# A linear-attention and mixture kernel: u spread by a bf16 product, no dummy products, another division of small work, and all orders anew

## The chip, the core and the metric

The kernel runs on one core of a Trainium2 chip. A core has five engines, each with an instruction queue of its own that it works through strictly in order: TensorE (PE, matrix products and transposes), VectorE (DVE), ScalarE (ACT), GpSimd (POOL) and SyncE (SP, which here only issues transfers). Transfers between the chip's main memory and the core's buffers, and transposes by transfer, run on 16 DMA engines that all queues share. The metric is the device time of one execution in microseconds (us).

## What is computed

Two stages follow each other. The first is a linear recurrence over 768 positions for 4 batches of 8 heads with 48 channels; the second is a feed-forward stage over the 3072 resulting rows of 384 numbers, with 1024 hidden columns.

```python
# first stage: r, k, v, w are [4, 8, 768, 48], u is [8, 48]; the state is [48, 48] per batch and head
for t in range(768):
    cur   = outer(u * k[t], v[t])
    y[t]  = r[t] @ (state + cur)
    state = w[t][:, None] * state + outer(k[t], v[t])
# second stage: x is y as [3072, 384]
h    = x @ w_in                                   # 1024 columns
solu = h * softmax(h)
ln   = (solu - mean(solu)) / sqrt(var(solu) + 1e-6) * g_ln
out  = ln @ w_out
```

The term with `u` is a bonus of each position for itself: the sum over the 48 channels of r·k·u, a single number per position and head, times the row v.

## The kernel before, in words

The positions are cut into 6 chunks of 128. A chunk of one batch is a **unit**; unit `i` is chunk `i // 4` of batch `i % 4`, so there are 24 units, and units 0 to 3 have no state behind them. For each unit the program does the following, and each step is one **word** in an order written out by hand:

- `LW`, `LK`, `LR`, `LV` load w, k, r and v of the unit (192 KB each). The ending of the word names the queue that issues the transfer: none is SP, `.a` is ACT, `.g` is POOL. `LI` and `LO` load the weights, `LU` and `LG` load u and the gain.
- `lw` (ACT) takes the logarithm of w, `cum` (PE, two products of 384 columns) sums it along the chunk, `ex` (ACT) takes exponentials, `kp` (DVE) multiplies them into k and r.
- The scaled k and r are turned, either by PE (`krk` and `krr`, eight transposes of 128 columns in all, copied out by `kr.a` on ACT or `kr.d` on DVE) or by a transfer (`kt`, issued by SP).
- `M` (PE) makes the scores, `m` masks them (DVE; `m.a` with `sel` in two units is ACT and POOL).
- `p` and `q` (POOL) make r·k and r·k·u; `dg` (DVE) sums q per head; `vb` casts v to bf16 on ACT or POOL; `dv` (POOL) multiplies the bonus by v.
- `Y` (PE) makes the attention output. With `.i` and a bank number, PE also adds `dv` by a product with the identity, and ACT copies the result out (`y.a`); with `.n`, DVE adds `dv` while it copies out (`y.d`).
- `S` (PE), `et` (ACT) and `st` (DVE) make the new state.
- y is turned, by PE (`X`, copied out by `xT.a` or `xT.d`) or by a transfer (`xt`, issued by SP).
- `H` (PE, 24 products of 128 columns) makes the hidden rows, `e` (ACT) exponentials, `he` (DVE) h·e, `hq` (ACT) its square. `Oa` and `Ob` (PE, four blocks each) multiply by w_out, and beside it sum the exponentials and the squares with products of two columns and one column. For units with `ea`, POOL first adds the two halves of the exponentials, which halves the number of those products. In units with `ht`, H is made by rows (six products of 512 columns), the two sums come from ACT's accumulators, and a transfer turns the result.
- `qm`, `lv`, `rs`, `o`, `out` normalise the rows and store them.

Before the first `H`, w_in must be cast to bf16 (`wi0` to `wi2`), and w_out must be scaled by the gain (`gw`) and centred (`mn`, `mc`, `ce`). `ih` and `ik` build constants. `hot` is a series of products whose result nobody reads.

What sets the order of the work is the string `ORDER` alone: it is walked word by word, and each engine gets its instructions in that order (class `InOrder`, lines 70 to 97; lines 680 to 683). An instruction that must wait therefore holds up everything behind it on its engine. A digit at the end of a PE word is the PSUM bank. Rings of buffers limit how far an engine can run ahead: seven loaded units, four to ten of the others (line 67). The trace has one line, 86, for nearly all instructions, because `InOrder.call` issues them; groups are told apart by the tiles that they write and read.

u is spread over all 128 rows by one product with a row of ones, in f32, before `q` can use it:

```python
u_row = consts.tile([1, DM], F32)                                                          # line 167
pe.matmul(ps["u"], lhsT=ones_row, rhs=u_row, start=True, stop=True)                        # us, line 279
act.copy(out=u_bc.rearrange("t h d -> t (h d)"), in_=ps["u"])                              # uc
```

Of the kernel before, what the change touches and what calls it, by code (L numbers as in the profile page):

```python
# [8 lines left out]
F32 = mybir.dt.float32  # L9
BF16 = mybir.dt.bfloat16  # L10
# [11 lines left out]
LU0 LR3.g LW3.a LW1.a LW2.g lw3 LR0.a cum3.0 LG0 ih0 ex3 LW0 gs0.7 LK3 LR2.g hot1.2 LV0.g ik0 LK0 lw1 lw0 LV3.g  # L22
gc0 cum0.4 LK2.a us0.6 p0 lw2 LW5.g ex0 kp3 LR1 kp0 cum1.0 cum2.2 krk3.7 krr3 uc0 ex2 q0 ex1 kp2 LK1 LR6.g kp1
krk0.6 LW4 krr0 krk2.5 krr2 kr0.a lw4 LR4.g vb0.a kr2.d vb3.a p1 M0.3 p3 LO0 LW6 dg0 M2.5 kr3.a LK4 m0.d lw5
hot10.1 LV1 LR5 LK6.a dv0 LK5.g m2.d LV2.a LO1 M3.0 S0.7 q3 gw2.a gw3.a hot1.4 LI1 q1 lw6 krk1.6 cum4.2 et0 LV4
m3.d p2 st0 cum6.0 dg3 gw0.a cum5.4 ex4 S3.7 gw1.a p4 kp4 q2 dv3 krr1 ex6 dg1 LV5.g krk4.3 krr4 ex5 vb1.a Y0.i2
kp6 kr4.d y0.a LI2 et3 X0.2 krk6.3 st3 p6 kr1.a vb2.a LW8 xT0.a kp5 krr6 LI0.a dg2 M1.0 krk5.7 krr5 kr6.a m1.d
S1.2 dv1 M4.4 dv2 Y3.i3 S2.6 gw4.a LK7 gw7.a et2 kr5.d LW7.g et1 m4.d hot1.7 y3.a gw5.a gw6.a p5 LR7.g M6.0
vb5.p Y2.i7 Y1.n3 vb4.a mn0.4 wi1.a y2.a st1 LW11.a wi0.p mc0 m6.d st2 S4.5 X3.2 LW10 y1.d et4 wi2.p ce0.d xT3.a
S5.0 ce5.p X1.7 LW9.a LV7.g et5 X2.6 M5.2 lw7 st5 st4 cum7.0 xT2.a H0.5 xT1.a LR10 lw8 ex7 m5.d ce1.d e0 H1.2  # L30
LR8 kp7 q5 he0 H3.0 q4 LV8.a ce3.p lw10 dg5 ce7.p ce6.p krk7.5 dg4 LK10 H2.6 LK8.a LV11 ce2.p krr7 LV6 e1 Y4.n4
he1 hq0.a LW13.a e3 e2 ce4.p dv4 he3 Oa0.3 cum10.1 he2 kr7.d y4.d Ob0 p7 cum8.6 qm0 lw11 hq1.a dv5 Oa1.0 ex10
Y5.n5 kp10 LR11 y5.d p8 LK11.a LK13 LW15 Ob1 X4.5 ex8 M7.1 lv0 krk10.4 rs0 kp8 q6 o0.a LK9.a vb6.p LW12 LR9 qm1
# [18 lines left out]
o11.a Oa10.5 kp20 e13 dv16 M17.0 out11 ea13.p he13 dg19 cum22.2 e15 p20 ex22 dv17 Y16.i4 he15 Ob10 kp22 y16.a
H14.6 hq13.a e14 qm10 LW23.g q20 p22 M18.3 dv18 q22 ea15.p S18.2 LV20 lv10 kt19 m17.d Y17.n1 m18.d hq15.a Oa13.0
y17.d et18 dg20 st18 Ob13 rs10 he14 M19.3 ea14.p o10.a xt16 vb20.p qm13 H16.1 e16 kt22 dv20 Y18.n6 X17.5 m19.d
lv13 kt20 y18.d out10 xT17.a q21 rs13 Oa15.7 LV22.g Ob15 he16 M20.4 qm15 hq14.a S17.3 lv15 m20.d H17.1 dg21 et17
st17 kt21 M21.5 dv19 rs15 LR23 o15.a e17 m21.d Oa14.4 Ob14 he17 lw23 o13.a qm14 cum23.5 Y19.n3 xt18 Y20.n7 ex23
y19.d lv14 out15 y20.d ht16 LV23 ea17.p vb22.p rs14 vb21.a o14.a H18.0 p23 e18 X20.2 dg22 M22.3 S19.7 hq17.a
kp23 xT20.d m22.d Oa16.6 sv16 dv21 Y21.n5 hq16.a sv18 vb23.a Ob16 sq16 et19 H20.2 out13 he18 q23 y21.d dg23 dv22
e20 st19 xt19 he20 H19.0 Y22.n5 Oa17.7 kt23 e19 dv23 qm16 Ob17 y22.d ht18 M23.4 xt21 he19 lv16 rs16 o16.d Oa18.3
Ob18 hq20.a H21.0 hq18.a hq19.a m23.d ht20 xt22 out14 sq18 sv20 qm18 e21 lv18 ea19.p Y23.n2 rs18 Oa19.6 qm17  # L60
ea21.p lv17 rs17 y23.d Ob19 he21 Oa20.5 hq21.a qm19 out16 H22.0 o17.d xt23 lv19 o18.d rs19 Oa21.2 HA23.3 Ob21
# [39 lines left out]
def kernel(  # L101
# [14 lines left out]
    C = 128  # L116
# [50 lines left out]
    u_row = consts.tile([1, DM], F32)  # L167
# [29 lines left out]
    ones_row = consts.tile([1, C], F32)  # L197
    dve.memset(ones_row, 1.0)
# [37 lines left out]
    u_bc = consts.tile([C, H, D], BF16)  # L236
    gr = consts.tile([128, KF], F32)
# [38 lines left out]
    def load_u(i, x):  # L276
        queue[x].dma_start(out=u_row, in_=u.rearrange("(o h) d -> o (h d)", o=1))
# [11 lines left out]

    def spread_u(i, x):  # L290
        ps["u"] = bank([C, DM], F32, x, "u_ps")
        pe.matmul(ps["u"], lhsT=ones_row, rhs=u_row, start=True, stop=True)
# [421 lines left out]
```

## Time and profile before

| | |
|---|---|
| median of three runs | 143.97 us (143.61 to 146.4) |
| the profiled execution | 142.83 us, of which the span of the trace is 141.0 us |
| PE busy | 125.5 us, 89% |
| DVE busy | 122.3 us, 87% |
| ACT busy | 118.9 us, 84% |
| POOL busy | 118.3 us, 84% |
| moved by DMA | 31.98 MB, 227 GB/s in the mean |

A group row of the trace reads: line, engine, operation, tiles out<-in, shapes, count | busy us, mean ns of one | idle time of the engine just ahead of them and what ended it. A row of the timeline reads: start, duration, engine, line, operation, tiles, count and, in brackets, the engine's wait ahead of it. Products are pipelined: the duration of one runs until its result has landed, so what a product costs a busy PE is read from start to start. All four engines are busy in more than eight tenths of the span, so a row's share says little; what matters is which of them the others wait for in a stretch.

### The profile page before, as it was taken

The page shows a single profiled execution, that of the slowest core. Times are in us where ns is not written, and L with a number is a line of the kernel's source. Part 1 is how long each engine was busy: PE and PEld are TensorE (multiplying, and loading weights), DVE is VectorE, ACT ScalarE, POOL GpSimd, SP SyncE. Part 2 cuts the span into 40 slices and gives each one's busy share as a digit, 9 for nine tenths or more (in the row PEclk, how much of TensorE's full clock was granted, in tenths as well). Part 3 has the DMA queues.
Part 4 walks back from the last instruction along what each step waited for, and adds up shares of the span by engine and source line. Part 5 has one row for each costly group of instructions (what it writes and reads, how often), then busy time and mean ns, then how long its engine had stood idle before and what let it go on. Part 6 is the DMA issues. An engine that isn't in the chain of part 4 may idle for free.

```text
span 141.0 us, 4797 instructions
## 1 busy us (share of the span) xinstructions
PE 125.5 (89%) x1890; PEld 94.6 (67%) x1890; DVE 122.3 (87%) x202; ACT 118.9 (84%) x243; POOL 118.3 (84%) x152
## 2 busy tenths in 40 slices
PE   0597956978999999999999999999999999999960
PEld 0136535657967887669877788788867766788740
DVE  6048879997999999999999998999999999878750
ACT  3648799979999999999989979998767889897780
POOL 7999999989999999999999999999999984402300
PEclk9999999999999999999999999999999999999996
DMA  4999999999999999999999999999999499652324
GB/s 89 274 298 343 323 278 388 382 307 232 263 234 237 285 297 295 242 227 223 297 190 238 188 242 213 291 224 162 186 228 213 97 255 86 144 170 78 123 73 154
DMA packets 94569, 31.98 MB, mean 227 GB/s; under 512 B 88569, under 2 KB 92674, under 8 KB 94546
## 3 DMA queue, kind: packets, MB, share of 16 engines
q1 hardware_dynamic: 70578, 20.92, 69.9%
q10 hardware_dynamic: 21984, 4.65, 15.6%
q0 software_dynamic: 1984, 6.10, 14.5%
q8 instruction: 15, 0.25, 0.8%
q14 instruction: 8, 0.07, 0.2%
HBM read 22.03 MB, written 4.72 MB: 190 GB/s over the span
## 4 chain that ended last, share of the span: by engine, by line
PE 40%; POOL 15%; DMA 13%; DVE 8%; ACT 5%; issue 2%; SPq 0%; ACTq 0%; POOLq 0%
PE ps L86 40%; DMA win_f<-in_moe_w_in_dram 5%; DMA kr_in<-in_k_dram 5%; DMA xT<-y 3%; POOL w L86 3%; POOL q L86 3%; DVE m L86 2%; POOL dv L86 2%; DVE he L86 2%; POOL m L86 2%; DVE y L86 1%; POOL win_sb L86 1%; ACT ps L86 1%; DVE kp L86 1%; POOL v_in L86 1%
## 5 line engine op out<-in xcount | busy, mean ns | idle before, releaser
L86 PE MATMUL ps<-w,he 128*128 128x386 bf16 (+1 forms) x192 | 43.2, 324 | 0.0
L86 PE MATMUL ps<-xT,win_sb 128*128 128x128 bf16 x504 | 31.2, 219 | 0.4 <-DMA xT<-y 0.2
L86 PEld LDWEIGHTS <-win_sb 128*128 128x128 bf16 x504 | 29.0, 98 | 2.1 <-DMA xT<-y 0.4
L86 ACT ACTIVATE e<-ps 128x1024 bf16<-128x1024 f32 (+1 forms) x25 | 24.6, 986 | 6.6 <-PE ps L86 5.0
L86 DVE TENSOR_TENSOR kp<-ps,kr_in 128x768 bf16<-128x768 f32 x24 | 22.7, 951 | 7.4 <-DMA kr_in<-in_r_dram 3.8
L86 PE MATMUL ps<-one_col,hq 128*128 128x1 bf16 x168 | 27.4, 163 | 0.0
L86 DVE TENSOR_TENSOR he<-ps,e 128x1024 bf16<-128x1024 f32 (+1 forms) x22 | 25.6, 1170 | 1.6 <-ACT e L86 1.3
L86 DVE TENSOR_TENSOR m<-ps,keep 128x1024 bf16<-128x1024 f32 x22 | 26.6, 1216 | 0.4 <-PE ps L86 0.4
L86 POOL TENSOR_TENSOR p<-kr_in 128x384 bf16<-128x384 f32 x24 | 24.0, 1004 | 0.3
L86 ACT ACTIVATE hq<-he 128x1024 bf16<-128x1024 bf16 (+1 forms) x21 | 21.6, 1030 | 0.7 <-DVE he L86 0.7
L86 POOL TENSOR_TENSOR q<-p,u_bc 128x384 bf16<-128x384 bf16 x24 | 21.7, 914 | 0.1
L86 POOL TENSOR_TENSOR dv<-vb,dg 128x384 bf16<-128x384 bf16 x24 | 19.8, 831 | 2.1 <-DVE dg L86 1.9
L86 ACT ACTIVATE ps<-ps 128x768 f32<-128x768 f32 x24 | 18.9, 796 | 2.6 <-PE ps L86 2.4
L86 PEld LDWEIGHTS <-he 128*128 128x128 bf16 x192 | 18.1, 96 | 3.5
L86 PEld LDWEIGHTS <-hq 128*128 128x128 bf16 x168 | 14.5, 96 | 8.8
L86 POOL TENSOR_TENSOR ea<-e 128x512 bf16<-128x512 bf16 x9 | 10.3, 1151 | 8.3 <-ACT e L86 8.3
L86 ACT ACTIVATE lw<-w_in 128x384 bf16<-128x384 f32 x24 | 12.3, 520 | 4.9 <-DMA w_in<-in_w_dram 4.9
L86 PE MATMUL ps<-inv_col,e 128*128 128x2 bf16 x96 | 15.8, 165 | 0.0
L86 PEld LDWEIGHTS <-kp 128*128 128x128 bf16 x176 | 11.8, 102 | 3.6 <-DVE kp L86 1.9
L86 PEld LDWEIGHTS <-kr 64*128 64x128 bf16 (+1 forms) x272 | 10.2, 95 | 5.3 <-issue 1.9
L86 DVE TENSOR_REDUCE dg<-q 128x8 f32<-128x384 bf16 x24 | 12.8, 544 | 0.2 <-POOL q L86 0.2
L86 DVE TENSOR_TENSOR st<-ps,et 128x384 bf16<-128x384 f32 x20 | 10.9, 549 | 0.6 <-ACT et L86 0.6
(97 smaller groups left out, 271.8 us busy)
## 6 DMA issues: line engine op xcount, KB each, us to landing
out_dram<-o SPq DMA_DIRECT2D x24, 192.0 KB, 3.7
kr_in<-in_k_dram SPq DMA_DIRECT2D x13, 192.0 KB, 5.8
kr_in<-in_r_dram POOLq DMA_DIRECT2D x12, 192.0 KB, 4.8
w_in<-in_w_dram SPq DMA_DIRECT2D x11, 192.0 KB, 5.2
kr_in<-in_r_dram SPq DMA_DIRECT2D x10, 192.0 KB, 4.8
v_in<-in_v_dram SPq DMA_DIRECT2D x10, 192.0 KB, 5.7
v_in<-in_v_dram POOLq DMA_DIRECT2D x9, 192.0 KB, 4.3
w_in<-in_w_dram ACTq DMA_DIRECT2D x8, 192.0 KB, 3.6
```

The lines of the kernel that those rows point to most:

```text
L86: made = make(*args, **kwargs)
```

## The change

- `us` becomes a bf16 product: u is loaded as 8 rows of 48, DVE multiplies it with the identity into a tile of 8 by 8 by 48 that holds u on its diagonal blocks (`ub`), and PE multiplies that with 8 rows of ones. u is also turned into columns (`uk`, three small transposes, and the copy `ud`). Words for a bonus sum by PE (`PT`, `pt`, `pd`, `DG`) are defined, but the order holds none of them.
- The five `hot` words, 15 products of 512 columns, are gone.
- Units 0 to 3 begin in the order 0, 2, 3, 1 instead of 3, 0, 2, 1 (order of `kp`: 0, 2, 3, 1; before 3, 0, 2, 1).
- Fourteen units have k and r turned by transfer (twelve before; units 8 and 10 are new); ten have y turned so, as before, with unit 20 in the place of unit 11.
- Five units (10, 11, 13, 14, 19) add the old state on DVE instead of by a PE product: an `S` with `.n` makes `st` two DVE instructions, one of which writes an f32 tile that the other reads. The code for that was there; no unit used it.
- Eight units have the bonus added by PE and y copied by ACT (four before).
- `ea` in eight units (nine before: 5 and 11 are out, 20 is in). `qa`, new, in units 15, 17, 19 and 21: POOL adds the two halves of the squares, which halves the products of one column. Unit 20 goes by columns like most, so `ht` is left in two units.
- Casts of v: 15 on POOL and 9 on ACT (10 and 14 before). Casts of w_in: one on POOL and two on ACT (two and one before). `xT`: six on DVE, eight on ACT (three and eleven). `o`: three on DVE, 21 on ACT (six and 18).
- Loads issued by SP 42, ACT 26, POOL 35 (before 50, 22, 31).
- The whole order is a new one.

```diff
 ORDER = """
...
-gc0 cum0.4 LK2.a us0.6 p0 lw2 LW5.g ex0 kp3 LR1 kp0 cum1.0 cum2.2 krk3.7 krr3 uc0 ex2 q0 ex1 kp2 LK1 LR6.g kp1
...
-hot10.1 LV1 LR5 LK6.a dv0 LK5.g m2.d LV2.a LO1 M3.0 S0.7 q3 gw2.a gw3.a hot1.4 LI1 q1 lw6 krk1.6 cum4.2 et0 LV4
...
-S5.0 ce5.p X1.7 LW9.a LV7.g et5 X2.6 M5.2 lw7 st5 st4 cum7.0 xT2.a H0.5 xT1.a LR10 lw8 ex7 m5.d ce1.d e0 H1.2
...
+LW1 LK3.g LW0.a LG0 gs0.3 LV0.g LU0 LW4 LW2.g LK0 LR0.a LW3.a LK2 gc0 LR2.g LR3.g lw0 cum0.0 LR1.g ex0 ub0 kp0
+us0.3 uc0 lw1 LK1.g uk0.0 lw2 LV2.a cum2.6 cum1.4 LR4.g ik0 lw3 ex2 p0 q0 kp2 cum3.2 ud0.d krk2.7 krr2 krk0.0
+LW5 ex3 ex1 lw4 kp3 LV3.g kr2.a LK4 krk3.2 krr3 kp1 LR5.a cum4.3 ex4 dg0 LK5.a p3 vb0.a LO0 krr0 kr3.d ih0 kr0.d
+LW6 vb2.a gw0.a LV4 LR6.g M2.1 kp4 S0.3 M0.5 krk1.7 p1 gw2.a LO1.a gw3.a m2.d LI0 LK6.g LI2.a m0.d krr1 q3 LV1.g
+LI1 et0 p2 LW8 S2.0 lw5 dg3 kr1.a M3.1 st0 m3.d vb3.a cum5.5 krk4.3 LV6.a S3.7 LW7.g ex5 et2 krr4 lw6 kr4.a dv0
+kp5 cum6.1 q2 et3 krk5.6 Y0.i4 ex6 dv3 y0.a krr5 M4.3 st2 Y3.i5 dg2 dv2 kr5.a p6 Y2.i0 st3 q1 gw6.a kp6 krk6.6
+krr6 vb4.p y3.a m4.d gw5.a y2.a X3.1 vb1.p dg1 LR7.a LV7.g X0.4 dv1 M1.2 kr6.d X2.5 m1.d S1.0 gw7.a M6.6 xT0.a
+xT3.d xT2.a p4 gw1.a et1 lw7 m6.d LV5 gw4.a Y1.n3 q6 y1.d LK7 mn0.2 wi0.a st1 wi1.a wi2.p LW13.a q4 p5 ce3.d
+M5.3 LR10 X1.6 cum7.0 LK9.a p7 xT1.d S4.5 LW12 ex7 LK11.a mc0 m5.d H0.6 et4 vb6.a LK10 LR11 lw8 e0 ce5.p ce6.p
...
+he13 dv18 ex20 H15.6 Oa10.5 cum22.3 S18.2 e15 ex22 et18 ea13.p q20 kp20 M17.0 Ob10 he15 H14.6 kp22 ea15.p hq15.a
+m17.d LK23.g hq13.a M18.3 kt19 e14 dg19 xt16 Oa13.0 Y17.i1 qm10 st18 Ob13 lv10 m18.d he14 LR23 vb22.p M19.3 rs10
+o10.a qa15.p dv19 y17.a m19.d qm13 H16.1 dg20 vb20.a e16 Y18.n6 kt20 Oa15.7 X17.3 M20.4 p21 p22 y18.d Ob15
+xT17.a lv13 S17.6 rs13 ea14.p hq14.a he16 kt21 o13.a et17 m20.d hq16.a kt22 Y19.n3 H17.1 qm15 q22 st17 lw23
+y19.d dv20 M21.5 m21.d p23 Oa14.4 e17 vb21.a out10 lv15 Y20.i3 he17 q21 y20.a xt18 dg22 Ob14 dg21 ea17.p rs15
+cum23.5 H18.0 ex23 kp23 o15.a M22.2 e18 qm14 LV23.g lv14 ht16 q23 m22.d dv21 S19.n7 xt19 dv22 hq17.a Y21.n5
+qa17.p he18 et19 xt20 rs14 sv16 Oa16.6 o14.a y21.d Ob16 H20.2 sq16 e20 dg23 H19.0 out13 st19 Oa17.7 sv18 ea20.p
+kt23 ht18 xt21 he20 out15 e19 ea19.p hq18.a Ob17 vb23.p qm16 he19 out14 Y22.n5 hq19.a lv16 M23.3 hq20.a qm17
+Oa18.2 y22.d Ob18 m23.d H21.0 rs16 qa19.p Y23.n3 dv23 e21 y23.d Oa20.5 Oa19.3 lv17 sq18 qm18 Ob19 rs17 xt22 lv18
...
-    u_row = consts.tile([1, DM], F32)
+    u_rows = consts.tile([H, D], F32)
...
-    ones_row = consts.tile([1, C], F32)
-    dve.memset(ones_row, 1.0)
+    ones_rows = consts.tile([H, C], BF16)
+    dve.memset(ones_rows, 1.0)
...
+    u_diag = consts.tile([H, H, D], BF16)
+    u_cols = consts.tile([128, KM, H], BF16)
...
+    def diagonal_u(i, x):
+        dve.tensor_mul(out=u_diag, in0=u_rows.unsqueeze(1).to_broadcast([H, H, D]),
+                       in1=ident_f[:H, :H].unsqueeze(2).to_broadcast([H, H, D]))
+
+    def turn_u(i, x):
+        ps["uk"] = bank([128, KM, H], BF16, x, "uk_ps")
+        for j in range(KM):
+            pe.transpose(ps["uk"][:, j, :], u_diag.rearrange("k h d -> k (h d)")[:, j * 128:(j + 1) * 128],
+                         ident[:H, :H])
...
     def spread_u(i, x):
         ps["u"] = bank([C, DM], F32, x, "u_ps")
-        pe.matmul(ps["u"], lhsT=ones_row, rhs=u_row, start=True, stop=True)
+        pe.matmul(ps["u"], lhsT=ones_rows, rhs=u_diag.rearrange("k h d -> k (h d)"), start=True, stop=True)
```

`qa` and the `.n` state are functions of the kernel before that its order does not call:

```python
def square_add(i, x):                                                                      # qa
    hq = hq_t[i % NWK]
    pool.tensor_add(out=hq[:, :KF // 2, :], in0=hq[:, :KF // 2, :], in1=hq[:, KF // 2:, :])
if live[i]["apart"]:                                                                       # st of an S with .n
    dve.tensor_add(out=sn_t[i % 2], in0=total, in1=st_t[b][(c - 1) % 2])
    total = sn_t[i % 2]
dve.tensor_mul(out=st_t[b][c % 2], in0=total, in1=et)
```

More of the change, by code (lines that the diff above doesn't have):

```diff
@@ L52 @@
[L52 to L61, printed above, removed]
@@ L276, in load_u @@
     def load_u(i, x):
-        queue[x].dma_start(out=u_row, in_=u.rearrange("(o h) d -> o (h d)", o=1))
+        queue[x].dma_start(out=u_rows, in_=u)
     def load_g(i, x):
@@ L288, in load_w_out, with copy_turned_u @@
                            in_=moe_w_out.rearrange("(ko ki) d -> ki ko d", ki=128)[:, part, :])
+    def diagonal_u(i, x):
[6 more added lines that the diff above has]
+                         ident[:H, :H])
+    def copy_turned_u(i, x):
+        copy = {"a": act.copy, "d": dve.tensor_copy}[x]
+        copy(out=u_cols, in_=ps["uk"])
     def spread_u(i, x):
         ps["u"] = bank([C, DM], F32, x, "u_ps")
[L292 removed]
+        pe.matmul(ps["u"], lhsT=ones_rows, rhs=u_diag.rearrange("k h d -> k (h d)"), start=True, stop=True)
     def copy_u(i, x):
```

75 lines of the change are left out of this document (45 added, 30 removed).

## The prediction

> **What bounds the kernel now.** I read the page first, for the engines, then the chain of waits in order of time.
>
> ```profile
> span 141.0 us, 4797 instructions
> ...
> PE 125.5 (89%) x1890; PEld 94.6 (67%) x1890; DVE 122.3 (87%) x202; ACT 118.9 (84%) x243; POOL 118.3 (84%) x152
> ```
>
> ```profile
> 23.15 6.93 DMA win_f<-in_moe_w_in_dram
> 30.08 0.05 issue
> 30.13 2.03 POOL win_sb L86 x2
> ...
> 82.33 54.11 PE ps L86 x822
> ...
> 137.26 0.58 ACT o L86
> ```
>
> No share stands out. The chain splits the span in two. Up to the first hidden product the end of the stage is set by the last piece of w_in and two POOL casts of it; from 82.33 to 136.44 us PE alone sets the end, and what follows PE's last product takes 141.0 - 136.44 = 4.6 us. The timeline of PE gives the start of the first hidden product and what products cost a busy PE, start to start:
>
> ```profile
> 10.00 0.53 PE L86 MATMUL ps<-lw,uts 128*128 128x384 bf16 x1
> ...
> 14.29 2.33 PE L86 MATMUL ps<-warm 128*128 128x512 bf16 x10
> ...
> 32.32 0.32 PE L86 MATMUL ps<-lw,uti_neg 128*128 128x384 bf16 x1 [1.33 <-ACT lw L86]
> 32.48 0.32 PE L86 MATMUL ps<-lw,uts 128*128 128x384 bf16 x1
> 32.64 4.18 PE L86 MATMUL ps<-xT,win_sb 128*128 128x128 bf16 x72
> 36.66 0.39 PE L86 MATMUL ps<-ident,kp 128*128 128x128 bf16 x4
> ...
> 41.27 0.33 PE L86 MATMUL ps<-w,he 128*128 128x386 bf16 x1
> 41.44 0.17 PE L86 MATMUL ps<-inv_col,e 128*128 128x2 bf16 x1
> 41.47 0.16 PE L86 MATMUL ps<-one_col,hq 128*128 128x1 bf16 x1
> 41.49 0.32 PE L86 MATMUL ps<-w,he 128*128 128x386 bf16 x1
> ```
>
> H0 starts at 32.64. 72 products of 128 columns take 36.66 - 32.64 = 4.02 us: 0.056 each, 1.34 a unit. A product of 384 columns takes 0.16 (32.32 to 32.48), one of 386 columns 0.17, one of two columns 0.03, one of a single column 0.02; a block of the output product 0.22 (41.27 to 41.49).
>
> POOL needs a closer look, because it is the engine that the change loads most. Its groups, and two rows of its timeline:
>
> ```profile
> L86 POOL TENSOR_TENSOR p<-kr_in 128x384 bf16<-128x384 f32 x24 | 24.0, 1004 | 0.3
> L86 POOL TENSOR_TENSOR q<-p,u_bc 128x384 bf16<-128x384 bf16 x24 | 21.7, 914 | 0.1
> L86 POOL TENSOR_TENSOR dv<-vb,dg 128x384 bf16<-128x384 bf16 x24 | 19.8, 831 | 2.1 <-DVE dg L86 1.9
> L86 POOL DMA_DIRECT2D kr_in<-in_r_dram x12 | 11.1, 921 | 0.3 <-POOL p L86 0.3
> L86 POOL TENSOR_TENSOR ea<-e 128x512 bf16<-128x512 bf16 x9 | 10.3, 1151 | 8.3 <-ACT e L86 8.3
> L86 POOL DMA_DIRECT2D v_in<-in_v_dram x9 | 8.2, 908 | 0.0
> L86 POOL CAST vb<-v_in 128x384 bf16<-128x384 f32 x10 | 4.9, 498 | 0.7 <-DMA v_in<-in_v_dram 0.6
> ...
> L86 POOL CAST win_sb<-win_f 128x1024 bf16<-128x1024 f32 x2 | 2.0, 1041 | 0.3 <-DMA win_f<-in_moe_w_in_dram 0.3
> ```
>
> ```profile
> 108.17 0.83 POOL L86 TENSOR_TENSOR dv<-vb,dg 128x384 bf16<-128x384 bf16 x1
> ...
> 119.49 0.83 POOL L86 TENSOR_TENSOR dv<-vb,dg 128x384 bf16<-128x384 bf16 x1 [1.95 <-DVE dg L86]
> ```
>
> The first is dv20, the second dv23. The idle column says that POOL waits for almost nothing but the exponentials of its `ea` (8.3 us, most of it behind dv23) and 1.9 us for one sum: up to about 109 us it runs without a pause, and it is free early only at the end. Its reserve before PE needs dv23 is the few microseconds behind 120.3. A load issued from POOL costs POOL 0.92 us.
>
> **The change part by part.**
>
> *u.* The f32 product becomes one of 0.16 to 0.53 us (its 384 columns at 32.48 and at 10.00). Nothing follows from it: around 8 us PE waits for w. The DVE product, the three small transposes and the copy are not in this trace; each costs between nothing and 0.55 us (the row of y below, a sum of the same 384 columns on all 128 rows). I take nothing, because POOL, not this, sets the start (next but one). Without that cover it is under 1.7 us.
>
> *Dummies.* 15 x 0.23 = 3.4 us of PE go, all ahead of H0, where PE has gaps. What is late next is POOL, so I count nothing here; what their absence may do to the clock is a rival below.
>
> *The start.* Ahead of the last cast of w_in, POOL's new order has two loads, one q and one cast of v more, and one p and one cast of w_in less: 2 x 0.92 + 0.91 + 0.50 - 1.00 - 1.04 = +1.2 us. The wait of 0.3 for w_in goes, since all three pieces are issued earlier. The cast ends at 32.16 + 1.2 - 0.3 = 33.1 and H0 starts there: +0.45. The casts on ACT, two instead of one, and the four more loads that ACT issues stand ahead of it; ACT has about 1.4 us to spare, an estimate from adding its words; were it gone, H0 would move with ACT's last cast.
>
> *PE from H0 on.* Sixteen transposes go (-0.9), five state products (-0.8), sixteen columns of squares (-0.3); four bonus products come (+0.65), four columns of exponentials (+0.1), and unit 20 by columns instead of rows (+0.4): -0.9 us. On PE alone the end would be +0.45 - 0.9 = -0.45.
>
> *DVE and ACT.*
>
> ```profile
> L86 DVE TENSOR_TENSOR y<-ps,dv 128x384 bf16<-128x384 f32 x20 | 10.8, 549 | 0.3 <-issue 0.3
> L86 DVE TENSOR_SCALAR qm<-ps 128x1 f32<-128x1 f32 x21 | 5.9, 281 | 0.9 <-PE ps L86 0.9
> L86 DVE COPY kr<-ps 128x1024 bf16<-128x1024 bf16 x8 | 5.5, 682 | 0.0
> ```
>
> DVE gets five state sums at about 0.55 and loses four sums of y (2.2) and two copies of kr (1.4); three o go to ACT and three xT come. That is a little under nothing. ACT trades five casts of v for four y, three o, a cast of w_in and fewer xT, of like size: about nothing. Neither is the bound. Two more turns by transfer go through SP's queue, which loses eight loads; I count nothing, with 1 us either way.
>
> *POOL, the term that decides.* Up to dv23 it gets four loads (3.7), five casts of v (2.5) and three `qa` at the price of `ea` (3.45), and loses one cast of w_in (1.0): +8.6 us. The 1.95 us wait and 0.9 of smaller ones fall away when POOL is late, so dv23 ends near 120.3 + 8.6 - 2.9 = 126.0. What hangs on it is y23, its turn and HA23:
>
> ```profile
> 125.99 0.56 DVE L86 TENSOR_TENSOR y<-ps,dv 128x384 bf16<-128x384 f32 x1 [0.30 <-issue]
> ```
>
> ```profile
> 130.15 0.83 PE L86 MATMUL ps<-xT,win_sb 128*128 128x128 bf16 x12
> ```
>
> From y23's start to HA23 are 4.2 us; 126.0 + 4.2 is 130.2, as before. The reserve is used up to the last tenth. Worse placed is qa15: Oa15 needs it on PE's queue. To its end the new order asks of POOL, compared with the old order to the end of dv20 (109.0): four loads, five casts of v and one `qa` more, and three `ea`, two p, one q, one dv and one cast less: 3.7 + 2.5 + 1.15 - 3.45 - 2.0 - 0.9 - 0.8 - 1.0 = -0.8. So qa15 is there at 108.2 (107.1 if POOL's small waits vanish). From Oa15 on PE has seven hidden stages (7 x 1.34 = 9.4), ten output stages (8 blocks at 0.22, or 0.17 in the two units by rows, less what `ea` and `qa` save: 15.5) and thirteen small pieces of about 0.35 (one `cum` takes 0.32: 4.6): 29.5 us. PE ends at 108.2 + 29.5 = 137.7, against 136.44: **+1.2 us**. A second place says the same: Y20 now takes dv20 on PE itself, and Ob14, cum23 and H18 stand behind it. Six instructions after qa15 (two dv, two p, one q, one `ea`: 5.7 us) dv20 is there at 113.9, and PE has 29.5 less H17, three output halves and five small pieces (1.3 + 2.4 + 1.6) to go: 24.2.
>
> *Sum.* 141.0 + 1.2 = 142.2 us of span, 144.0 us in the profiled execution (142.83 before), +0.8%. The median of the runs shown is 143.97, 0.8% above the profiled execution; scaled alike I forecast **145.1 us**. About 2%, 2.9 us, is what can be told from no change.
>
> **The rivals.**
>
> *PE stays the bound.* If POOL's waits and issue times overlap more than I take, the end is at -0.45 us: 143.5. For it speaks that 54 us of the chain are PE; against it the sum for POOL. If PE's remaining hidden stalls went too (its products from H0 on add up to about 101 us by the paces above, an estimate, in 103.8 us of time), another 2.7 us would go: 140.8, the one case that is faster by 2%.
>
> *POOL and DVE collide.* The `.n` state multiplies two SBUF tiles on DVE (an f32 sum and the decays), which no state does before. If POOL stands still meanwhile, the price is up to 5 x 0.55 = 2.7 us of POOL, paid in full at Oa15, since POOL has nothing left: 145.1 + 2.7 = 147.8, slower. It decides from the first such unit, 10. The Trainium skill's GPSIMD Engine Reference, section Key points, says that POOL shares its SBUF interfaces with VectorE and contends with DVE instructions that have two SBUF inputs; no row of this trace shows that at work.
>
> *PE runs at half pace in the start.* The same product of 384 columns takes 0.53 us at 10.00 and 0.32 at 32.48: early products were slow here. The dummies at 14.29 kept PE busy for 2.3 us. If without them PE stays at half pace until H0, its work behind the first kp, about 12 us by these paces (an estimate), doubles and ends near 35.5 instead of 33.1: +2.4 on the PE path, that is 143.5 + 2.4, and up to 1.3 more if H0 itself, 1.34 us, starts slow: 146 to 148. The Trainium skill's TensorE: Matmul & The Clock Gate, Part 1, says that half rate is the default, released by about 3.4 us of sustained work and lost after as long an idle window. The trace agrees that the early products are slow; by that rule the removal costs time only if a gap of 3.4 us opens, and the longest gap before H0 once products are fast is the 1.33 us in the row of 32.32.
>
> *The change does not unload PE.* One-column products cost PE 0.02 us, not the 0.16 of their rows; `qa` then buys 0.3 us of PE for 4.6 us of POOL. This is inside my sum already.
>
> **How the numbers follow.** POOL sets the end: 0.50, 144.0 to 146.5. PE stays the bound: 0.24, of which 0.07 under 141.1. POOL collides with DVE: 0.14, 146 to 148. Slow start: 0.12, 146 to 148. That puts 0.07 on faster by over 2%, 0.65 on within 2%, 0.28 on slower (most of the last two rivals and the upper end of the first case, where DVE falls behind because it waits for dv). The range runs from the middle of the PE case to the end of the two slow ones: 142.8 to 148.2.
>
> **What would show it.** Right: POOL's idle column for `ea` shrinks, POOL is busy without a pause to about 126 us and its total is near 127 us; H0 starts near 33; PE shows waits for POOL at Y20, Oa15, Oa14 or Oa17. Wrong: POOL waits in the middle (then its sum was not the bound), p or q rows above 1.05 us (collision), products of 384 columns at 0.5 us beyond 20 us (slow start), or H0 more than 1 us from 33.

## The result, and the profile after

The changed kernel takes 148.65 us in the median (147.29 to 149.85) against 143.94 us of the kernel before in the same session (143.61 to 146.4): the ratio of undisturbed runs is 1.0257, with a 95% interval of 1.0206 to 1.0309. It is slower by 2.6%; a rise of 0.8% was forecast. The profiled execution took 147.29 us, its span is 145.6 us. First the page of the changed kernel:

```profile
span 145.6 us, 4786 instructions
...
PE 124.3 (85%) x1880; PEld 95.3 (65%) x1882; DVE 123.2 (85%) x203; ACT 118.9 (82%) x239; POOL 127.0 (87%) x163
...
PEclk9999996869999999999999999999999999999999
```

POOL's total is the 127 us of the forecast. PE's is 1.2 us lower, less than the forecast's parts make (3.4 us of dummies and 0.9 us behind H0): ahead of H0, where the dummies are missing, PE is busy for 21.5 us instead of 22.5, only 1.0 less, because part of its products run at half pace there. New are the 6, 8 and 6 in the row of PE's granted clock, between 22 and 33 us. The longest pieces of the chain of waits in that stretch (start, length):

```profile
16.86 11.98 DMA wout_f<-in_moe_w_out_dram
29.90 4.39 PE ps L85 x46
```

Not a cast of w_in, as before, but the second half of w_out leads to the first hidden product. PE's timeline has the stations to compare with 32.64 and 130.15 in the kernel before (H0 and HA23; the second row is cut off where the view ends):

```profile
29.90 0.78 PE L85 MATMUL ps<-ident,y 128*128 128x128 bf16 x6 [2.46 <-ACT y L85]
...
35.83 1.34 PE L85 MATMUL ps<-xT,win_sb 128*128 128x128 bf16 x21
...
132.80 1.50 PE L85 MATMUL ps<-xT,win_sb 128*128 128x128 bf16 x24 [0.80 <-DVE he L85]
...
134.95 1.50 PE L85 MATMUL ps<-xT,win_sb 128*128 128x128 bf16 x24
```

| | before | after | difference |
|---|---|---|---|
| H0 starts | 32.64 | 35.83 | +3.19 |
| H0 to HA23: work of PE | 93.9 | 92.8 | -1.1 |
| H0 to HA23: waits of PE | 3.6 | 6.3 | +2.7 |
| HA23 to the end of the span | 10.85 | 10.65 | -0.2 |
| span | 141.0 | 145.6 | +4.6 |

Work and waits of PE are parted by spacing: for each kind of piece on PE (a `cum`, an `M`, an output half and so on), the time from its start to the next piece's start; the lower quartile of a kind times its count is work, what lies above it is wait. How the kinds are cut moves about 0.3 us between the two rows. So in this trace two thirds of the loss stand ahead of H0, and the rest are small waits behind it. This says where the time lies, not what a repair of one part would bring: e11 below repairs the start and loses most of the lead again.

**Ahead of H0.** ACT's timeline of the changed kernel:

```profile
25.12 1.01 ACT L85 COPY kr<-ps 128x1024 bf16<-128x1024 bf16 x1
28.87 0.61 ACT L85 ACTIVATE w<-wout_f,gr 128x384 bf16<-128x384 f32 x1 [2.73 <-DMA wout_f<-in_moe_w_out_dram]
...
29.39 0.46 ACT L85 CAST y<-ps 128x384 bf16<-128x384 f32 x1
29.75 0.61 ACT L85 ACTIVATE w<-wout_f,gr 128x384 bf16<-128x384 f32 x1
30.26 0.46 ACT L85 CAST y<-ps 128x384 bf16<-128x384 f32 x1
```

The gain `gw6` waits 2.73 us for the second half of w_out, which lands at 16.86 + 11.98 = 28.84. Behind it stand the copies of y3 and y2, whose products ended on PE at 26.6 and 27.0; PE waits for them from 27.4 to 29.90, and M1, S1, mn0, M5 and X1 stand behind on PE. In the kernel before, the gains of the second half (`gw4`, `gw7`) could run 3.6 us earlier:

```profile
25.26 1.16 ACT L86 ACTIVATE w<-wout_f,gr 128x384 bf16<-128x384 f32 x2
```

**Behind H0.** The largest wait is the one of 0.80 us ahead of H22 in PE's timeline (0.95 by the spacing). The timeline of DVE and POOL shows where it is from:

```profile
130.44 1.16 POOL L85 TENSOR_TENSOR ea<-e 128x512 bf16<-128x512 bf16 x1 [0.75 <-ACT e L85]
...
130.55 1.06 DVE L85 TENSOR_TENSOR qm<-s,sq 128x1 f32<-128x1 f32 x1 [0.27 <-ACT sq L85]
...
131.54 1.21 DVE L85 TENSOR_TENSOR he<-ps,e 128x1024 bf16<-128x1024 f32 x1
```

`qm18` works on a single column, takes 1.06 us and ends with POOL's addition; `he21`, whose bank H22 needs, stands behind it. The groups, by shape:

```profile
L85 DVE TENSOR_TENSOR st<-ps,et 128x384 bf16<-128x384 f32 x15 | 8.2, 546 | 0.0
...
L85 DVE TENSOR_TENSOR st<-sn,et 128x384 bf16<-128x384 f32 x5 | 3.2, 641 | 0.2
L85 DVE TENSOR_TENSOR sn<-ps,st 128x384 f32<-128x384 f32 x5 | 2.7, 549 | 0.1
L85 DVE TENSOR_TENSOR qm<-s,sq 128x1 f32<-128x1 f32 x2 | 1.2, 606 | 0.3 <-ACT sq L85 0.3
```

A state with its sum on DVE costs 641 + 549 ns there instead of 546. Other waits of PE behind H0, each for DVE, stand ahead of M9 (0.80), Y16 (0.55) and Oa13 (0.24), by the spacing. With H22 these are 2.5 of the 6.3 us; the rest is spread over many pieces.

### The profile page after: what moved, and what is told of

Same layout as the page of the kernel before. It is cut to its first block, busy times and chain, and to the rows that moved or that the text cites. A ratio compares the mean times of both kernels' runs of the same rounds, so it can differ in the third digit from the quotient of the medians.

```text
span 145.6 us, 4786 instructions
## 1 busy us (share of the span) xinstructions
PE 124.3 (85%) x1880; PEld 95.3 (65%) x1882; DVE 123.2 (85%) x203; ACT 118.9 (82%) x239; POOL 127.0 (87%) x163
## 4 chain that ended last, share of the span: by engine, by line
PE 30%; POOL 21%; DMA 16%; ACT 11%; DVE 11%; issue 7%; ACTq 2%; POOLq 0%; DVEq 0%
PE ps L85 30%; DMA wout_f<-in_moe_w_out_dram 8%; POOL p L85 5%; DMA kr_in<-in_r_dram 4%; POOL dv L85 4%; DVE he L85 4%; DMA w_in<-in_w_dram 3%; ACT e L85 3%; POOL kr_in L85 3%; POOL q L85 2%; DVE m L85 2%; POOL v_in L85 2%; DVE kp L85 2%; ACTq L85 2%; ACT lw L85 2%
## 5 line engine op out<-in xcount | busy, mean ns | idle before, releaser
L85 PE MATMUL ps<-xT,win_sb 128*128 128x128 bf16 x528 | 32.2, 219 | 0.8 <-DVE he L85 0.8
L85 PEld LDWEIGHTS <-win_sb 128*128 128x128 bf16 x528 | 30.2, 98 | 2.0 <-issue 1.0
L85 DVE TENSOR_TENSOR m<-ps,keep 128x1024 bf16<-128x1024 f32 x22 | 26.6, 1214 | 2.7 <-PE ps L85 2.6
L85 DVE TENSOR_TENSOR he<-ps,e 128x1024 bf16<-128x1024 f32 (+1 forms) x23 | 26.6, 1169 | 0.5 <-ACT e L85 0.4
L85 PE MATMUL ps<-one_col,hq 128*128 128x1 bf16 x160 | 26.1, 163 | 0.0
L85 ACT ACTIVATE hq<-he 128x1024 bf16<-128x1024 bf16 (+1 forms) x22 | 22.4, 1031 | 0.6 <-DVE he L85 0.5
L85 PE MATMUL ps<-inv_col,e 128*128 128x2 bf16 x112 | 18.4, 165 | 0.0
L85 PEld LDWEIGHTS <-kr 64*128 64x128 bf16 (+1 forms) x272 | 11.3, 99 | 5.8 <-issue 3.5
L85 PEld LDWEIGHTS <-kp 128*128 128x128 bf16 x160 | 11.0, 106 | 5.0 <-DVE kp L85 2.5
L85 ACT ACTIVATE o<-ps,rs 128x384 f32<-128x384 f32 x21 | 11.9, 575 | 0.5 <-ACT rs L85 0.3
L85 PE MATMUL ps<-kr 64*128 64x128 bf16 x192 | 10.7, 231 | 0.9 <-DVE m L85 0.7
```

Of the source, the lines that this page charges most:

```text
L85: made = make(*args, **kwargs)
```

## The experiments

Three theories were set against each other. W: the late half of w_out and the order of ACT's words make the start late, and PE keeps that to the end. C: the missing dummies let the clock fall, and this makes the start late. P: POOL, which the change loads most, sets the end. All runs were beside the kernel before on the same chip.

### e1: the dummies back

```diff
-m3.d vb3.a cum5.5 krk4.3
+m3.d vb3.a cum5.5 hot2.4 krk4.3
-kp5 cum6.1 q2
+kp5 cum6.1 hot3.4 q2
-krr6 vb4.p
+krr6 hot8.1 vb4.p
```

> The changed kernel with 13 dummy products put back into three gaps of PE ahead of H0 (2, 3 and 8 products of 512 columns). Theory C, the clock costs the start: the granted clock stays at 1.0 through 23 to 34 us, the PE stretch from 29.9 to 35.8 us shrinks by 1.7 us, H0 starts near 34.1 and the end comes 1.7 us earlier. Theory W, the late second half of w_out holds ACT's queue: the clock stays full, but H0 waits for ACT's second cast of w_in, which ended at 35.55, so H0 comes at 35.5 or later and the time gains at most 0.3 us. Theory P, POOL sets the end: no change of the end.

Measured: 147.88 us, ratio 1.0283 (1.0223 to 1.0342). Its page and its timeline of PE:

```profile
PEclk9999999999999999999999999999999999999999
```

```profile
35.55 0.67 PE L85 MATMUL ps<-xT,win_sb 128*128 128x128 bf16 x9
```

In this row the clock is full throughout, and H0 gains 0.28 us. So in the profiled execution of the changed kernel the clock is not what made the start late: PE at half pace lay beside ACT, which was busy from 28.87 to 35.5 without a pause. The ratio is no better than the changed kernel's 1.0257, and from H0 to HA23 e1 takes 100.1 us against 99.1, though its order is the same there: four of its five `.n` states took 0.83 to 1.21 us on DVE instead of 0.56 (more below, under the rivals).

The clock is not always harmless. The orders of e6 and e10 below are the changed kernel's up to H0, and in their profiled executions the clock was at half from 28.45 to 35.27 and from 28.80 to 35.62. There ACT's last cast of w_in ended at 35.31 and 35.13, but PE was still working through the column mean and what stands behind it, and H0 came at 36.63 and 36.66: 1.1 us later than in e1. So C holds for up to 1.1 us of the start in some executions; in the time no run shows it.

### e8: the kernel before without its dummies

```diff
-hot1.2  hot10.1  hot1.4  hot1.7  hot2.0
```

> The kernel before without its 15 dummy products, nothing else changed: that part of the change alone. Theory C (dummies hold the clock): the granted clock falls to half in one or more windows of about 3.4 us between 12 and 33 us, the early products run at 0.5 us instead of 0.32, and H0 comes up to 1.7 us later than 32.64; the time rises by as much. Otherwise: clock full from about 16 us on, H0 at 32.64 as before because POOL's cast of w_in sets it, time unchanged within 0.5 us.

Measured: 143.39 us against 143.51, ratio 0.9984 (0.9944 to 1.0023). The view by windows (window, its length, busy time of each engine, granted clock, DMA share, GB/s):

```profile
16.00:18.00 2.00, 1.64 (x23) 0.90 (x17) 2.00 (x2) 1.30 (x3) 1.98 (x3) 0.67 1.15 311
18.00:20.00 2.00, 1.38 (x5) 0.65 (x5) 1.05 (x3) 2.00 (x6) 2.00 (x3) 0.50 1.29 269
...
24.00:26.00 2.00, 2.00 (x24) 1.61 (x22) 2.00 (x3) 2.00 (x5) 2.00 (x3) 0.50 1.11 352
26.00:28.00 2.00, 2.00 (x45) 1.57 (x43) 1.91 (x3) 1.04 (x4) 1.98 (x3) 0.77 1.10 359
```

PE ran at half pace for 10.2 us (16.70 to 26.94), against 6.8 us in the changed kernel, H0 started 0.64 us later, at 33.28, and the time did not change. In the kernel before, taking the dummies out costs nothing and brings nothing.

### e2 and e3: one repair of the start each

The first diff is e2, the second e3.

```diff
-gw2.a LO1.a gw3.a m2.d LI0 LK6.g
+gw2.a LI0.a gw3.a m2.d LO1 LK6.g
```

```diff
-q1 gw6.a kp6
+q1 kp6
-y3.a m4.d gw5.a y2.a X3.1
+y3.a m4.d y2.a gw6.a gw5.a X3.1
```

> The changed kernel with two transfers exchanged: SP issues the second half of w_out where it issued the first third of w_in, ACT the reverse. Theory W: the half of w_out lands some 3 to 5 us earlier (28.85 in the changed kernel), ACT's wait of 2.73 us for it goes, H0 starts near 33.1 and the end comes about 2.7 us earlier. Theory C: the clock still falls to half for want of dummies, H0 gains 1 us at most. Theory P: H0 moves, but qa15 and dv20 on POOL end within 1.1 us of where they did (109.8 and 115.3 us; 1.1 is POOL's one wait for the mean of w_out), and the end moves by no more.

> The changed kernel with two words moved on ACT: the copies of y3 and y2 stand ahead of the gains gw6 and gw5 instead of behind them; the transfers stay. Theory W: y3 and y2 are copied near 26.6 us, PE's wait of 2.46 us before the transposes of y shrinks below 1 us, but ACT still waits for w_out until 28.9 and has 5.7 us of work from there to its second cast of w_in: H0 near 34.9, the end 0.9 us earlier. Theory C: as PE's gap closes, the clock does not fall at 30 us and 0.5 to 1 us more goes. Theory P: the end moves by 1.1 us at most.

Measured: e2 150.5 us, 1.0387 (1.0318 to 1.0455); e3 148.5 us, 1.0311 (1.0238 to 1.0384). Neither did what it was meant to. In e2 SP issued the half at 14.16, but with w_in on both queues beside it the half still landed only at 28.4: the edit did not test W. In e3 the transposes of y began at 28.21, 1.7 us earlier, but the column mean stood ahead of H0 on PE, waited 0.8 us for the gains and ran in part at half clock; H0 came at 36.29. (e3 also began its first transposes 1.4 us later, behind a `kp` that waited for a load.)

### e4: e1 and e2 together

> The edits of e1 and e2 together. Theory W: H0 near 33.0, where POOL's cast of w_in ends, as in e2; end 2.7 to 2.9 us earlier than in the changed kernel, about 145.5 us in the median, so still behind the kernel before by what PE waits later. Theory C: 1.5 us better than e2. Theory P: no more than 1.1 us better than the changed kernel.

Measured: 150.48 us, 1.0309 (1.0211 to 1.0406), H0 at 38.15 in the profile, after PE had waited 3.25 us for kp5, which waited for a load of k. As e2 missed its aim, this says nothing on W; it shows only that a single late load moved the start.

### e5: the start repaired by moving words

```diff
-q1 gw6.a kp6
+q1 kp6
-krr6 vb4.p y3.a m4.d gw5.a y2.a X3.1
+krr6 hot4.1 vb4.p y3.a m4.d y2.a wi0.a X3.1
-S1.0 gw7.a M6.6
+S1.0 wi1.a gw6.a gw5.a gw7.a M6.6
-xT2.a p4 gw1.a
+xT2.a wi2.p p4 gw1.a
-LK7 mn0.2 wi0.a st1 wi1.a wi2.p LW13.a q4 p5 ce3.d
+LK7 st1 LW13.a q4 p5
-mc0 m5.d H0.6 et4 vb6.a LK10 LR11 lw8 e0 ce5.p
+m5.d H0.6 mn0.2 et4 vb6.a LK10 LR11 lw8 e0 mc0 ce3.d ce5.p
```

with five more dummies (hot2.4 and hot3.4) where e1 has them.

> The changed kernel with its order repaired ahead of H0 alone: the copies of y3 and y2 and the two ACT casts of w_in stand ahead of the gains that wait for the second half of w_out, POOL's cast of w_in stands one p earlier, the column mean (PE) and its copy stand behind H0, and nine dummies fill PE's gaps. Theory W (the loss is made ahead of H0): H0 starts near 33 instead of 35.83 and the end comes 2.5 to 3 us earlier, about 145.5 us in the median against 143.9 of the kernel before. Theory P (POOL sets the end, whatever H0 does): H0 moves as much, but POOL gains only its one wait of 1.1 us for the mean, the products wait later for dv or for what hangs on it, and the end gains 0 to 1.1 us.

Measured: 150.95 us, 1.0486 (1.0424 to 1.0548). H0 started at 34.12, 1.7 us earlier, but the lead was gone at H1 (37.59, against 37.17 in the changed kernel): H0 ran at half clock until 35.82, and the mean now stands behind it. H3 came later still (40.29 against 38.51), by the edit itself, as DVE's timeline shows:

```profile
38.30 0.61 DVE L85 SCALAR_TENSOR_TENSOR w<-wout_f,gr,ps 128x384 bf16<-128x384 f32 x1 [3.86 <-ACT mean_sb L85]
38.83 0.54 DVE L85 TENSOR_REDUCE dg<-q 128x8 f32<-128x384 bf16 x1
39.29 0.95 DVE L85 TENSOR_TENSOR kp<-ps,kr_in 128x768 bf16<-128x768 f32 x1
```

The centring that the edit puts ahead of kp7 waits for the mean, and H3 waits for kp7. Moving the mean only moves the wait as long as w_out is late.

### e6: POOL relieved, the start left

```diff
-qa15.p  qa17.p  qa19.p  qa21.p
-LV14.g  LK21.g  LR19.g  LV18.g
+LV14    LK21    LR19    LV18
```

> The changed kernel with POOL relieved and the start left as it is: the four additions of squares are out (PE takes the sixteen columns again, +0.3 us) and four loads in the middle (v14, k21, r19, v18) are issued by SP: 8.3 us less on POOL, all of it behind 60 us. Theory P: the end comes earlier by 1.5 to 2.5 us, the stalls of PE behind H0 (5.2 us) fall to about those of the kernel before (2.7). Theory W: PE from H0 on has 100.5 us of work, so at most the same 2.5 us can go, and the 3.2 us lost ahead of H0 stay: 146 at best.

Measured: 149.85 us, 1.0434 (1.0378 to 1.0489). Its page:

```profile
PE 125.5 (85%) x1896; PEld 96.0 (65%) x1898; DVE 124.4 (84%) x203; ACT 118.9 (80%) x239; POOL 118.9 (80%) x155
```

POOL has 8.1 us less to do, and stands idle for 10 us more; PE gains nothing, its waits for DVE ahead of M9, Y16 and H22 are there as before. Its start, which the edit does not touch, came 0.8 us later in the profiled execution (under e1), and from H0 to HA23 it took 100.2 us against 99.1; by its ratio it is slower than the changed kernel. It is not a clean test: four of its five `.n` states took 0.77 to 1.30 us on DVE, 1.8 us above 0.56 each in sum, against 0.4 in the changed kernel, and this can hide a gain of about that difference. But with 8.1 us off POOL, no gain shows and no wait of PE for POOL was there to be removed. Behind 60 us POOL does not set the pace of the changed kernel by more than that: P falls for that stretch as the main cause.

### e7: e5 and e6 together

> The edits of e5 and e6 together. If the loss has two independent parts (3.2 us ahead of H0, 2.5 us of stalls behind it), the gains add: 4 to 5 us, about 143.5 us, level with the kernel before or just under it. Theory P alone: no better than e6. Theory W alone: no better than e5.

Measured: 151.4 us, 1.0456 (1.0386 to 1.0526): no better than e5, whose error it carries.

### e9: the start repaired by the order of the loads

```diff
-gw2.a LO1.a gw3.a m2.d LI0 LK6.g LI2.a m0.d krr1 q3 LV1.g LI1 et0 p2 LW8
+gw2.a gw3.a m2.d LO1 LK6.g m0.d krr1 q3 LV1.g LI0 et0 p2 LI1 LW8
-LW7.g ex5 et2
+LW7.g ex5 LI2.a et2
-q1 gw6.a kp6
+q1 kp6
-y3.a m4.d gw5.a y2.a X3.1
+y3.a m4.d y2.a gw6.a gw5.a X3.1
-S1.0 gw7.a M6.6 xT0.a xT3.d xT2.a p4 gw1.a et1 lw7 m6.d LV5 gw4.a Y1.n3 q6 y1.d LK7 mn0.2 wi0.a st1 wi1.a wi2.p LW13.a q4 p5 ce3.d
+S1.0 gw7.a gw1.a gw4.a M6.6 xT0.a xT3.d xT2.a wi2.p p4 et1 lw7 wi0.a m6.d LV5 wi1.a Y1.n3 q6 y1.d LK7 mn0.2 st1 LW13.a q4 p5
-ex7 LK11.a mc0 m5.d H0.6
+mc0 ex7 LK11.a m5.d ce3.d H0.6
```

> The changed kernel with the stretch ahead of H0 repaired in another way than in e5, where the copy that centres w_out on DVE was put ahead of kp7 and held it: the second half of w_out is issued by SP ahead of all of w_in, w_in follows it on SP and ACT; on ACT the copies of y3 and y2 come first, then all gains, then the casts of w_in; the mean keeps its place on PE. No dummies. Theory W+PE (the late half of w_out costs the start, and from H0 on PE is the bound, so that lateness is kept to the end, as the constant shifts of e5 and e6 against the changed kernel suggest): w_out lands before 25 us, H0 starts near 33.2, and the end comes 2 to 2.6 us earlier than the changed kernel's: 146 to 146.6 us in the median. If transfers as a whole (9.8 MB in the first 36 us of both kernels) set the pace, not their order: H0 moves by less than 1 us, because then w_in or the k and r of unit 7 are late instead.

Measured: 149.57 us, 1.0405 (1.0337 to 1.0473). w_out landed at 25.01 as meant, but H0 came at 35.77. ACT's timeline:

```profile
21.15 0.51 ACT L85 CAST vb<-v_in 128x384 bf16<-128x384 f32 x1
23.91 0.37 ACTq L85 DMA_DIRECT2D v_in<-in_v_dram  x1
24.38 0.80 ACT L85 ACTIVATE ps<-ps 128x768 f32<-128x768 f32 x1 [2.72 <-DMA kr_in<-in_k_dram]
```

The exponentials do not read k. What waited is the issue of v6 ahead of them, and it waited until the load of k5 had landed, at 23.88. The pattern is in the changed kernel too: its load of k7 is issued at 28.92, just after the half of w_out has landed at 28.84, the first piece of w_in to be issued last at 19.47 after r5 at 19.45, w8 at 22.36 after k5 at 22.28. In each pair the two stand eight places apart in the order of the loads that SP and ACT issue. On SP such a wait holds only later loads; on ACT it holds everything.

### e11: e9 with that wait taken away

```diff
-LR5.a cum4.3 ex4 dg0 LK5.a p3
+LR5.a cum4.3 ex4 dg0 LK5 p3
-lv17 sq18 qm18 Ob19 rs17 xt22 lv18 ea21.p xt23 rs18 he21 o16.a o18.a o17.d qm19 hq21.a
+lv17 sq18 Ob19 rs17 xt22 ea21.p xt23 he21 qm18 o16.a o17.d qm19 lv18 rs18 o18.a hq21.a
```

> The edits of e9 and the later place of qm18 of e10 (without its other part), and the load of k5 issued by SP instead of ACT. In the traces of the changed kernel and of e9, a load issued by SP or ACT starts only when the one eight places before it in the order of those two queues has landed (v6 at 23.91 after k5 had landed at 23.88 in e9), and on ACT that held the exponentials of unit 5 for 2.72 us. If that is what undid e9: ACT's wait goes, k5 lands near 13 us, kp5 ends near 23 instead of 26.2, H0 starts near 33.3 and PE keeps that to the end; with 0.8 us from the end of the order, the span is about 3.3 us shorter than the changed kernel's 145.6: 142.3, some 145.3 us in the median. If the sum of the transfers sets H0 whatever their order, H0 is at 34.5 us or later and only the 0.8 us at the end are gained.

Measured: 147.07 us, 1.0209 (1.0099 to 1.032). The timeline of PE:

```profile
33.18 2.84 PE L85 MATMUL ps<-xT,win_sb 128*128 128x128 bf16 x48
...
36.73 2.84 PE L85 MATMUL ps<-xT,win_sb 128*128 128x128 bf16 x48 [0.71 <-DVE kp L85]
...
42.11 0.32 PE L85 MATMUL ps<-w,he 128*128 128x386 bf16 x1 [0.41 <-POOL w L85]
...
53.12 0.32 PE L85 MATMUL ps<-dv,ident 128*128 128x384 bf16 x1 [0.45 <-POOL dv L85]
```

H0 starts at 33.18, 2.65 us earlier than in the changed kernel, with all its work and without dummies. The clock differs too (full from 22.19 on here), but against e1, where it is full as well, it is still 2.37 us. So the start could have been what was forecast, and the order of the loads and of ACT's words, taken together, had cost about 2.4 us: the first half of W is shown. The second half is not: by 54 us the lead is down to 0.6 us, and by 113 us to 0.1 (a hidden stage starts at 113.32 here and at 113.45 in the changed kernel). First PE waits for kp7, whose k lands at 34.92; then for POOL, which runs without a pause from 32.5 to 101 us and itself is only 0.5 us ahead of the changed kernel. It has the six centrings done at 42.06 (39.60 in the kernel before) and dv7 at 53.07 (50.94). Here, in the first 20 us behind H0, P is right: POOL stands just behind the start as the next limit. What takes the last 0.5 us, between 54 and 113 us, was not tested. The median is 1.6 us lower than the changed kernel's; the intervals overlap, so the gain in time is not shown.

### e10: the state sums back on PE, qm18 behind he21

```diff
-S11.n4  S10.n1  S13.n3  S14.n1  S19.n7
+S11.4   S10.1   S13.3   S14.1   S19.7
```

with the second part of e11's edit.

> The changed kernel with two parts taken out that its trace keeps apart. First, the five state sums on DVE go back to PE: PE gets 5 x 0.163 = 0.8 us more, DVE 2.75 us less. If DVE holds PE up between 60 and 110 us, the waits for DVE at the scores of units 16 to 18 (0.55 and 0.24 us) vanish and the two sides cancel; if not, the end is 0.8 us later. Second, at the end, qm18 (two SBUF inputs) is moved behind he21. Collision theory: qm18 took 1.06 instead of 0.15 us because POOL's addition of exponentials ran beside it; with it gone he21 starts 0.9 to 1.1 us earlier and PE's wait of 0.80 us ahead of H22 vanishes. Rival: he21 is slowed in its place or waits for its exponentials, and H22 waits as before.

Measured: 147.5 us, 1.0274 (1.0211 to 1.0337). The timeline of DVE and POOL at the end:

```profile
130.84 1.22 DVE L85 TENSOR_TENSOR he<-ps,e 128x1024 bf16<-128x1024 f32 x1
130.88 1.16 POOL L85 TENSOR_TENSOR ea<-e 128x512 bf16<-128x512 bf16 x1 [0.74 <-ACT e L85]
131.98 0.15 DVE L85 TENSOR_TENSOR qm<-s,sq 128x1 f32<-128x1 f32 x1
```

qm18 takes 0.15 us, he21, which reads PSUM and one SBUF tile, is not slowed beside the same addition, and PE's wait ahead of H22 is gone: the collision is shown, 0.95 us of PE. With the sums on PE, its work from H0 to HA23 is 0.7 us more than in the changed kernel, its waits are 2.1 us less (4.2 against 6.3): those ahead of Y16, Oa13 and H22 have vanished, and one of 0.62 us for a turning transfer is new at 62.42. That makes H0 to HA23 97.8 us, against 99.1, and 97.5 in the kernel before. In time nothing shows (1.0274 against 1.0257); in the profiled execution H0 lay at 36.66, 0.83 us later than in the changed kernel, at half clock (under e1).

### e12: small edits to the kernel before

```diff
-hot1.2  hot10.1  hot1.4  hot1.7  hot2.0
-vb2.a LW8 xT0.a
+vb2.a LW7 xT0.a
-kr5.d LW7.g et1
+kr5.d LW8.g et1
-et4 wi2.p ce0.d
+et4 wi2.d ce0.d
```

> The kernel before with small edits that the traces point to, to beat both: no dummies (one of them cost PE 0.43 us behind H0), one of POOL's two casts of w_in on DVE, which waits there, and the loads of w for units 7 and 8 exchanged. H0 was set by POOL's second cast (32.16) and by cum7, which waited for that w (32.32). If PE keeps from H0 on what it has at H0: H0 near 31.8 instead of 32.64 and the time 0.8 to 1.2 us shorter, 142.7 to 143.1 in the median. If not, unchanged.

Measured: 144.21 us against 143.86, ratio 1.0 (0.9959 to 1.0042). H0 was at 33.73 in the profile, not at 31.8: no version was found that beats the kernel before. Why its start did not move was not followed up.

## What held of the prediction and what failed, point by point

Scaled like the forecast, the ratio gives 143.97 x 1.0257 = 147.7 us, inside the range of 142.8 to 148.2, near its end; the plain median of 148.65 lies just above it. That the range holds it at all is luck: its upper end was meant for a collision that costs POOL time and for a slow clock, and neither made the loss in that way. "Within 2%", given 0.65, did not come, and neither did the main case, that POOL sets the end.

- **u, the bf16 product.** Right: the DVE product took 0.55 us from 4.75 on, and kp0 behind it waited for its k (landed at 7.02) anyway.
- **Dummies, at nothing.** Right in the time (e8: 0.9984; e1: no gain), not in every execution's start. The rival on the clock described what happened, half pace and 384 columns in 0.5 us behind 20 us, but its price of 2.4 us was too high: 0.28 us in the profiled execution of the changed kernel, 1.1 us in those of e6 and e10. It was cited that the rate is lost after an idle window of about 3.4 us; here it fell sooner. The changed kernel by windows, cut where its clock changes:

```profile
16.30:19.70 3.40, 2.11 (x50) 1.63 (x44) 3.40 (x4) 3.40 (x9) 3.36 (x5) 1.00 1.24 283
19.70:23.15 3.45, 2.00 (x25) 1.05 (x21) 3.06 (x5) 3.43 (x8) 3.41 (x4) 1.00 1.06 385
23.15:26.56 3.41, 3.15 (x35) 2.26 (x36) 3.05 (x6) 1.95 (x3) 3.41 (x5) 0.50 1.04 377
26.56:29.98 3.42, 0.96 (x20) 0.72 (x18) 1.84 (x3) 1.11 (x3) 3.40 (x6) 1.00 1.16 323
29.98:33.39 3.41, 3.41 (x44) 2.47 (x45) 2.12 (x3) 3.33 (x9) 3.41 (x5) 0.50 1.16 256
```

  The first number behind the comma is PE's busy time, the last but two the clock. Full pace is followed by half after a window with 2.00 us of work, and not after one with 2.11. The steps of 3.4 us agree with the Trainium skill's TensorE: Matmul & The Clock Gate, Part 1; that a whole window must be idle does not: the longest wait of PE that touches the window from 19.70 was 0.85 us. The other runs put the edge at about 2 us of work in 3.41 as well, but not sharply: full pace was lost after 2.17 us (e3, from 29.21) and kept after 2.04 (e5, from 22.16).
- **The start, +0.45.** This is the step that failed: +3.19. Its POOL part was right (last cast at 32.95, forecast 33.1). Wrong was "ACT has about 1.4 us to spare", worked out by adding ACT's words: the sum left out that `gw6` would wait 2.73 us for a load, with y3 and y2 behind it. That w_in is issued earlier was taken as a gain, without asking what it does to w_out beside it. e11 shows the same work reaching H0 at 33.18.
- **PE from H0 on, -0.9.** Right: -1.1.
- **DVE and ACT, about nothing.** Right as a total (DVE 122.3 and 123.2 us), wrong as a conclusion: five sums cost DVE 3.2 us, PE waits for DVE, and e10 shows 2.1 us of waits gone without the sums and without the collision, for 0.7 us of PE.
- **POOL, the term that decides.** The total was right, the point at which it binds was not. qa15 ended at 109.80 (forecast 108.2) because POOL waited 1.84 us for what the late start held up, and Oa15 started at 110.51 without waiting for it. Of the places named, Y20, Oa15, Oa14 and Oa17, PE waited for POOL at none. Oa15 came only 0.7 us behind qa15, and the start was 2.7 us later than forecast: whether POOL would have bound at Oa15 with the start as forecast is not shown. Without POOL's late load (e6) nothing is won; with the start repaired (e11) POOL binds between 40 and 54 us.
- **The rivals.** "PE stays the bound" was the mechanism behind H0, with a start 2.7 us and waits 2.7 us worse than it assumed. "POOL and DVE collide" was right in kind and wrong in the side that pays: POOL's p and q rows kept their 1.00 and 0.91 us, it is DVE that stood still, 0.97 instead of 0.56 us in one of five `.n` states and 0.9 us at qm18, which was not forecast. That it was only one of five is chance: in e1, e5 and e6, which have the same five, it was four of five, with 0.77 to 1.30 us. Each state of these runs that began well inside a `q` or `dv` of POOL ended 0.42 to 0.43 us behind the end of that operation (in e5, 100.39 + 1.30 = 101.69, and POOL's q ended at 101.27), and qm18 ended with POOL's addition; beside a load that POOL issues, some states were slowed and some not. The Trainium skill's GPSIMD Engine Reference, Key points, names DVE instructions with two SBUF inputs; both of these have two, and he21 with one was not slowed.
- **The sum.** 142.2 us of span against 145.6: 2.7 of the 3.4 us are the start. The rest is a balance: the 1.65 us of waits for POOL that lie in the forecast (+1.2 instead of -0.45) did not come, and 2.7 us of other waits did, of which the largest are for DVE; PE's work and the end came out 0.2 us lower each.

Open: the wait of 0.8 us ahead of M9, which no edit moved; and whether e11 with POOL relieved and the sums on PE would reach the kernel before, which was not tried. e11 shows the cause of the late start and e10 most of the waits behind it, each on PE's timeline; that the two together make the 2.6% is added up, since no run took both away.

## What to carry to other kernels

When a change moves loads, follow every consumer on the queue of a compute engine, not only the operand that the change is about: one late transfer holds all words behind its first reader. Where all engines are busy in 85% and more, a bound found at one place does not absorb waits at others; add PE's own waits along its whole order. Two executions of one order can differ by 1 us in a stretch through the clock or through what DVE happens to meet on POOL: compare more than one profile before an edit is given the credit. Take the total of an engine and its place on the path apart: three totals here were forecast to 1 us, and the time was not.

## What the hardware showed that was not expected

A load issued by SP or ACT started only when the one eight places before it in their common order had landed (19.47 after 19.45, 22.36 after 22.28, 28.92 after 28.84, and in e9 23.91 after 23.88), and on ACT such an issue held the computation behind it for 2.72 us. In the three pairs of the changed kernel the trace gives both loads the same semaphore (105, 106, 102), so the wait is one of the program; that the chip itself needs it is not shown. The second half of w_out took 7.3 us to land in the kernel before (17.87 to 25.21, with two pieces of w_in behind it on the same queue), and 12.0 us in the changed one (16.86 to 28.84, issued by ACT, with w_in on both queues beside it):

```profile
wout_f<-in_moe_w_out_dram SPq DMA_DIRECT2D x2, 768.0 KB, 7.3
```

```profile
wout_f<-in_moe_w_out_dram ACTq DMA_DIRECT2D x1, 768.0 KB, 12.0
```

The first row is of the kernel before, the second of the changed one, both from the view of the transfers between 5 and 36 us; the columns are size and time from issue to landing. The x2 counts both halves, but only the second has a landing in the trace. With w_in on both queues and the half on SP, in e2, it took 14.2 us (14.16 to 28.4); with w_in behind it on SP and one later piece on ACT, 9.7 us in e9 and 8.5 us in e11.
